# A gated H3 convolution and shifted-MLP mixer on one core: transposes moved to DMA, sums and table arithmetic spread over ScalarE and GpSimd, a filter input moved to another buffer, the instruction order tuned anew

## The chip, the cores and the metric

The kernel runs on one core of a Trainium2 chip. The metric is the device time of that core in microseconds (us). Before the change it is 277.49 us, the median of three runs (275.71 to 279.33).

The engines are called as the profile calls them: PE is TensorE (matrix products, and transposes done as products with an identity matrix), PEld its weight loads, DVE is VectorE, ACT is ScalarE, POOL is GpSimd, and SP is SyncE, whose queue starts the DMA transfers. "L547" is line 547 of the kernel in question. Line numbers differ between kernels, so each reading says what the line does.

A run counts as slow when it is more than 1.5% above the fastest run of the same kernel.

## The reference

Inputs are sequences of S = 2048 positions with D = 640 channels, in bf16. Two branches are mixed by a gate.

```python
g = sigmoid((q * gate_w).sum(-1, keepdims=True))
# branch a: H3 convolution
k_shift = sum over t of k shifted by t * shift_k        # 4 taps
kv  = k_shift * v
y   = irfft(rfft(pad(kv)) * rfft(pad(ssm_k)))[:S] + kv * ssm_D
a   = q * y
# branch b: MLP with token shifts
h   = gelu(layernorm(q) @ w1)                           # layer norm 1
hs  = concat(shift of four channel groups by +1, -1, +2, -2) @ w2
x1  = q + hs
b   = x1 + gelu(layernorm(x1) @ w3) @ w4                # layer norm 2
out = g * a + (1 - g) * b
```

## The kernel before

The Fourier transform is done as products in two steps. Step 1 multiplies 16 slabs (a slab is 128 positions by 640 channels) by a table of sines `F1`, once for the filter (`h1`) and once for `kv` (`x1`). Step 2 multiplies by a small table `M3`; then come the spectral products, the inverse of step 2 (`pv`) and the inverse of step 1 (`iv`, with the table `I1`, which is `F1` transposed). "The last spectral product" below means the last matmul of step 2 and its inverse. What follows it, called the tail here, is the inverse `iv`, the rest of W3 and W4, and the stores.

A small list scheduler, which runs while the kernel is built, decides in which order each engine executes all this. Every operation has an estimated duration and a rank. The rank is the latest start that the work behind it allows, lowered to a hand-set target time where there is one. Where an operation has alternatives (`{V: ..., A: ...}`), the scheduler chooses the engine too.

```python
LAT = 70.0                     # ns between an end and the start that depends on it, any pair of engines
TG = {"trh": us(lambda a: 4 + a), "W1": us(lambda c: 10 + 6 * c), "h1": us(lambda s: 24 + 1.2 * s),
      "W3": us(lambda c, f: 50 + 36 * c + 1.5 * f), "W4": us(lambda c, i: 70 + 36 * c + 4 * i), ...}   # cut
n.rank = min((s.rank - LAT for s in n.succ), default=400000.0) - dur
if n.tgt is not None:
    n.rank = min(n.rank, n.tgt)
```

Layer norm: the sums of a slab, then mean and 1/sqrt for two slabs at a time, the normalised slab `XN`, and its transposition to `XNT` as PE products, two slabs (10 transposes) at a time.

```python
def ln_slab(i, s, dep):                                  # i = 0: layer norm 1, i = 1: layer norm 2
    if i == 0:   # VectorE: two bn_stats and one bn_aggr
        st = pl.add("st", {V: 2 * dve(DH) + 200}, f_st, dep)
    else:        # ScalarE: Square with accum_out (the plain sum came with the W2 addition)
        st = pl.add("sq", {A: act_s(D) + 60}, ..., dep)
    # i == 1: three small VectorE operations (mean, variance); then two on GpSimd: + 1e-5, pow(-0.5)
    xn = pl.add("xn", {V: 360}, ...)                     # (x - mean) * rs
def ln_pair(i, c, i0, xns, xb):                          # both layer norms
    tr = pl.add("tr", {PE: 10 * 66}, f_tr, ...)          # nc.tensor.transpose x10
    return evac("te", ...)                               # PSUM -> XNT, on ScalarE or VectorE
```

The buffers that matter:

```python
KV  = big.tile([P, T1, D], BF16)                         # v slabs, then kv
RK  = big.tile([P, 12800], BF16)
HT  = RK[:, 0:10240]                                     # the filter, transposed: input of h1
KRG = RK[:, 0:8960]; ACC = RK[:, 8960:10240]             # k slabs and sums of the four-tap shift
TMP = RK[:, 10240:12800]
kb  = Buf(r_kr, hpe)                                     # k loads wait for every filter product (hpe)
```

So `k` cannot be loaded, and the four-tap shift products on VectorE cannot begin, before all 32 filter products of step 1 are done. (The name `HT` means the transposed filter and not its spectrum; the wording of the prediction, "spectra in the value slabs", means this buffer.)

The rest that the change touches: the token shifts of the mixed channels (`mx`) are copies on VectorE. The twiddle transposes (`tri`, `F1` to `I1`) are 32 PE transposes and two copies out of PSUM, the memory that PE writes to. The scalings of the residual (`xo`), the angles of the sine table and the mask tables are all on VectorE.

## Time and profile before

| Reading | Value |
|---|---|
| Time, median of three runs | 277.49 us |
| Span of the profiled run | 275.1 us |
| PE busy | 231.0 us |
| DVE busy | 222.9 us |
| PE idle before / after the last spectral product | 28.7 / 15.4 us |

The page's first parts, before: busy time of each engine with its share of the span, then busy tenths in 40 equal slices (one slice is 6.9 us), where `PEclk` is the granted PE clock in tenths.

```profile
span 275.1 us, 4562 instructions
PE 231.0 (84%) x1757; PEld 136.2 (50%) x1757; DVE 222.9 (81%) x419; ACT 148.5 (54%) x182; POOL 25.9 (9%) x59
...
PE   3479989799999999989989789978989699992950
...
PEclk9999999999999999999999999999999999998695
```

PE is busy for 84% of the span. It cannot finish earlier than its 231 us of work, and 44 us beside that are idle. The row `PE` shows where: at the start, in the 70% slices, and in a hole near the end (2, 9, 5, 0), where the clock falls as well.

Windows of the kernel before: start and end, length, then busy time and instruction count of PE, PEld, DVE, ACT and POOL, the granted clock, the DMA share and GB/s. The first two lines split the run at the last spectral product, at 231.95 us.

```profile
0.00:231.95 231.95, 203.25 (x1588) 119.05 (x1589) 198.67 (x382) 146.93 (x181) 25.86 (x59) 1.00 0.61 214
231.95:275.10 43.15, 27.74 (x171) 17.18 (x170) 24.20 (x37) 1.53 (x2) 0.00 (x0) 0.85 0.75 259
94.00:120.00 26.00, 24.82 (x168) 15.70 (x166) 25.62 (x42) 11.01 (x17) 3.94 (x5) 1.00 0.37 115
```

Ahead of the split PE works 203.25 of 231.95 us, so 28.7 us are idle. Behind it PE has only 27.74 us of work, and this takes 43.15 us: 15.4 us are idle. The third line is the stretch of the shift products, where DVE is busy for 25.62 of 26.00 us.

Groups of instructions, before, by line and shape: busy us, mean ns of one, then the idle time just before them with its releaser.

```profile
L547 PE MATMUL PS<-IDN,XN 128*128 128x128 bf16 x160 | 12.3, 225 | 2.0 <-DVE XNT L348 1.9
L842 PE MATMUL PS<-IDN,F 128*128 128x128 bf16 x32 | 2.1, 219 | 0.1
...
L512 DVE BATCH_NORM_STATS2 ST<-QX 128x6 f32<-128x320 bf16 x32 | 13.6, 467 | 0.0
...
L516 ACT ACTIVATE RG<-QX 128x640 bf16<-128x640 bf16 x16 | 11.8, 736 | 11.8 <-DVE QX L684 10.4 <-issue 1.4
...
L530 POOL TENSOR_TENSOR RS<-VE,NHALF 128x2 f32<-128x2 f32 x16 | 12.7, 797 | 1.3
```

These price what moves: 160 layer-norm transposes cost PE 12.3 us (80 of them, 6.15 us, belong to layer norm 2), the twiddle transposes 2.1 us. One summing pass over a slab costs ScalarE 736 ns, one `pow` costs GpSimd 797 ns.

### The profile page before, as it was taken

Reading aid. Unit: us, or ns where it says so; the run is one execution under the profiler, and the core shown is the slowest. Engines: PE = TensorE matmul, PEld = TensorE weight load, DVE = VectorE, ACT = ScalarE, POOL = GpSimd, SP = SyncE. Lnnn points to the kernel's source line nnn. Section 1 sums busy time; section 2 is a strip of 40 time slices with the busy share of each in tenths; the row PEclk is TensorE's granted clock in tenths of the full one; section 3 lists DMA queues with packets and bytes.
Section 4 is the critical chain, followed back from the end, with each engine's and each line's share of the span. In section 5 each row is a group of like instructions: output and inputs, shape, how many; then the busy total and the mean of one; then the engine's idle time right before and its main releaser. Section 6 shows DMA issues by size and latency. Waiting matters only on the chain.

```text
span 275.1 us, 4562 instructions
## 1 busy us (share of the span) xinstructions
PE 231.0 (84%) x1757; PEld 136.2 (50%) x1757; DVE 222.9 (81%) x419; ACT 148.5 (54%) x182; POOL 25.9 (9%) x59
## 2 busy tenths in 40 slices
PE   3479989799999999989989789978989699992950
PEld 4465455456664546754456543334645244761620
DVE  6989999959988999999999595999488926164694
ACT  1479969987765461374632384889276964100000
POOL 6143220010520221100000000000000000000000
PEclk9999999999999999999999999999999999998695
DMA  7999604069990040492043999959959610699954
GB/s 261 397 362 299 257 2 191 2 223 386 396 355 26 2 167 0 133 324 96 31 162 89 354 342 297 357 204 313 377 149 387 222 67 0 200 389 379 339 150 166
DMA packets 32790, 60.90 MB, mean 221 GB/s; under 512 B 2305, under 2 KB 19458, under 8 KB 32385
## 3 DMA queue, kind: packets, MB, share of 16 engines
q1 hardware_dynamic: 32768, 60.63, 62.9%
q8 instruction: 13, 0.21, 0.3%
q14 instruction: 9, 0.07, 0.1%
HBM read 37.03 MB, written 18.35 MB: 201 GB/s over the span
## 4 chain that ended last, share of the span: by engine, by line
PE 48%; DVE 26%; DMA 10%; ACT 9%; issue 5%; SPq 1%; POOL 0%; DVEq 0%; ACTq 0%; POOLq 0%
PE PS L763 17%; PE PS L775 14%; PE PS L580 4%; DMA CJ<-in_A_q_dram 4%; DMA RK<-in_A_k_dram 3%; DMA RK<-GHD 3%; PE PS L677 3%; PE PS L731 3%; PE PS L856 3%; DVE RK L823 2%; DVE W L426 2%; DVE SX L348 2%; ACT RG L767 2%; ACT SX L344 2%; DVE QX L781 2%
## 5 line engine op out<-in xcount | busy, mean ns | idle before, releaser
L775 PE MATMUL PS<-W,RG 128*128 128x320 bf16 x384 | 56.0, 305 | 2.0 <-DVE SX L348 1.1
L763 PE MATMUL PS<-XNT,W 128*128 128x512 bf16 x240 | 54.1, 379 | 1.7 <-ACT RG L767 1.0
L344 ACT CAST SX<-PS 128x640 bf16<-128x640 f32 (+1 forms) x56 | 41.1, 784 | 22.6 <-PE PS L731 22.5
L775 PEld LDWEIGHTS <-RG 128*128 128x128 bf16 x384 | 38.3, 100 | 19.3 <-issue 3.6
L763 PEld LDWEIGHTS <-W 128*128 128x128 bf16 x240 | 23.2, 98 | 30.4 <-issue 4.8
L767 ACT ACTIVATE RG<-PS 128x1024 bf16<-128x1024 f32 x24 | 24.5, 1022 | 22.5 <-PE PS L763 22.3
L781 DVE SCALAR_TENSOR_TENSOR QX<-PS,ZG,QX 128x640 bf16<-128x640 f32 x16 | 14.1, 882 | 19.8 <-PE PS L775 19.8
L348 DVE CAST SX<-PS 128x640 bf16<-128x640 f32 (+1 forms) x28 | 24.9, 903 | 1.0 <-PE PS L856 1.0
L677 PE MATMUL PS<-R 128*128 128x320 bf16 x160 | 24.0, 299 | 0.9 <-DVE ZG L606 0.3
L916 DVE TENSOR_TENSOR SX<-SX,R 128x2048 bf16<-128x2048 bf16 x20 | 23.8, 1220 | 0.7 <-PE PS L856 0.5
L580 PE MATMUL PS<-XNT,R 128*128 128x512 bf16 x100 | 22.2, 379 | 0.0
L827 DVE TENSOR_TENSOR RK<-RK 128x1280 bf16<-128x1280 bf16 x24 | 19.7, 822 | 0.5
L856 PEld LDWEIGHTS <-M 64*64 64x64 bf16 x320 | 8.9, 105 | 22.1 <-issue 14.6
L677 PEld LDWEIGHTS <-R 128*128 128x128 bf16 x160 | 15.6, 98 | 8.2 <-issue 2.0
L823 DVE TENSOR_TENSOR RK<-RK,CJ 128x1280 bf16<-128x1280 bf16 x24 | 19.6, 818 | 0.0
L731 PEld LDWEIGHTS <-F 128*128 128x128 bf16 x128 | 12.3, 97 | 12.2 <-issue 7.3
L344 ACT COPY XNT<-PS 128x1280 bf16<-128x1280 bf16 x13 | 16.0, 1232 | 4.0 <-PE PS L547 3.9
L516 ACT ACTIVATE RG<-QX 128x640 bf16<-128x640 bf16 x16 | 11.8, 736 | 11.8 <-DVE QX L684 10.4
L344 ACT CAST KV<-PS 128x1024 bf16<-128x1024 f32 x14 | 14.1, 1023 | 7.4 <-PE PS L856 7.2
L856 PE MATMUL PS<-RK,M 64*64 64x512 bf16 x160 | 13.4, 387 | 5.4 <-DMA RK<-GHD 2.4
L957 DVE SCALAR_TENSOR_TENSOR RK<-PS,ZG,CJ 128x640 bf16<-128x640 f32 x16 | 13.3, 877 | 4.4 <-DMA CJ<-in_A_q_dram 4.4
L350 DVE TENSOR_SCALAR R<-PS 128x1024 bf16<-128x1024 f32 x11 | 13.0, 1219 | 4.7 <-PE PS L856 4.5
(95 smaller groups left out, 299.1 us busy)
## 6 DMA issues: line engine op xcount, KB each, us to landing
GHD<-SX SPq DMA_DIRECT2D x8, 640.0 KB, 5.4
GXD<-SX SPq DMA_DIRECT2D x8, 640.0 KB, 3.3
RK<-GHD SPq DMA_DIRECT2D x4, 1280.0 KB, 8.8
R<-R SPq DMA_DIRECT2D x8, 640.0 KB, 8.0
RK<-GXD SPq DMA_DIRECT2D x4, 1280.0 KB, 7.6
VD<-KV SPq DMA_DIRECT2D x4, 1280.0 KB, 6.1
RK<-VD SPq DMA_DIRECT2D x8, 640.0 KB, 5.9
W<-in_B_w_dram SPq DMA_DIRECT2D x2, 1920.0 KB, 11.2
```

The costliest lines, as they stand in the source:

```text
L344: nc.scalar.copy(out=o, in_=i)
L348: nc.vector.tensor_copy(out=o, in_=i)
L580: nc.tensor.matmul(ps(pb)[:, j, :], lhsT=lhsT, rhs=XNT[:, xb.idx, k, :], start=(k == 0), stop=(k == DT - 1))
L677: nc.tensor.matmul(ps(pb)[:, j, 0:DH], lhsT=gst_ap(k, s), rhs=W2[:, k, j * DH:(j + 1) * DH], start=(k == 0), stop=(k == DT - 1))
L731: nc.tensor.matmul(ps(pb)[:, j, 0:DH], lhsT=F1[:, s, h, :], rhs=src[:, s, ds], start=True, stop=not dterm)
L763: nc.tensor.matmul(ps(pb)[:, j, :], lhsT=W3[:, k, (f0 + j) * P:(f0 + j + 1) * P], rhs=XNT[:, xb.idx, k, :], start=(k == 0), stop=(k == DT ...
L767: gns.append(pl.add("g2.%d.%d" % (c, f0), {A: act_p(1024)}, lambda e, f0=f0, pb=pb, gb=gb: nc.scalar.activation(out=GTP[:, gb.idx, f0 % 4: ...
L775: nc.tensor.matmul(ps(pb)[:, j, 0:DH], lhsT=GTP[:, gbs[f // 4].idx, f % 4, i * P:(i + 1) * P], rhs=W4[:, f, j * DH:(j + 1) * DH], start=(f ...
L823: m = pl.add("km%d.%d.%d" % (c, u, j), {V: dve(2 * D, .52)}, lambda e, src=src, cj=cj, tb=tb: nc.vector.tensor_tensor(out=TMP[:, tb.idx].r ...
L827: prev = pl.add("ka%d.%d.%d" % (c, u, j), {V: dve(2 * D, .52)}, lambda e, tb=tb: nc.vector.tensor_tensor(out=acc, in0=acc, in1=TMP[:, tb.i ...
L856: nc.tensor.matmul(pt[64 * C:64 * C + 64, R, :], lhsT=M3[64 * R:64 * R + 64, m, :], rhs=rhs_fn(R, C), start=start, stop=stop)
L916: nc.vector.tensor_tensor(out=PQ[:, qb.idx], in0=XS[:, sb.idx].unsqueeze(1).to_broadcast([P, 2, 1024]), in1=HH[:, hhb.idx, u], op=ALU.mult)
```

## The change

The intent is to relieve PE and VectorE, the two busiest engines, with engines that have room (ScalarE at 54%, GpSimd at 9%, the DMA queue at 62.9% of its engines' time):

- Layer norm 2's 80 transposes and the 32 twiddle transposes become DMA transposes. Layer norm 1 keeps PE transposes.
- Layer norm 1's sums may run on ScalarE (two summing passes) or VectorE, as the scheduler picks. The mean and variance of layer norm 2 go to GpSimd.
- Angles may run on GpSimd, and so may the copies of the shift coefficients; the mask tables do. The scalings `xo` may run on ScalarE.
- The token shifts of the mixed channels become small DMA copies.
- The transposed filter `HT` moves from `RK` into `KV`, so `k` loads and shift products no longer wait for the filter products. The `v` loads now wait for them instead.
- The scheduler changes too: other hand-over latencies, a new target for the `kv` products, four settings (`keep`, `evac`, `vpen`, `mpen`), and targets whose odd values look like the result of a search.

The diff, cut to its core (cuts marked `...`):

```diff
-LAT = 70.0
+def lat_of(n):
+    return 230.0 if "PE" in n.alts else (60.0 if n.bytes else 170.0)
...
-    TG = {"trh": us(lambda a: 4 + a), "W1": us(lambda c: 10 + 6 * c), ... }
+PAR = {
+    "trh": (-602.97, -1.2), "W1": (-11.87, 12.07, -4.15), "h1": (-36.96, 5.52), "W2": (1.53, 2.52),
+    "W3": (284.34, -0.66, -0.95), "W4": (27.62, 66.24, 29.05), "x1": (225.73, -0.37), "h2": (309.29, 2.1, 1.28),
+    "x2": (430.37, -0.29, 0.64), "pv": (93.48, 0.63, 0.03), "iv": (205.62, 6.17), "kv": (376.91, -0.47),
+    "keep": (0.07,), "evac": (1.85,), "vpen": (43.36,), "mpen": (14.32,),
+}
...
+    XTD = {(1, c) for c in range(4)}
+    LN1A = {s for s in range(T1)}
-    HT = RK[:, 0:10240].rearrange("p (t d) -> p t d", t=T1)
+    HT = KV
...
-            st.append(pl.add("ang%d" % t1, {V: dve(256)}, ...
+            st.append(pl.add("ang%d" % t1, {V: 397, G: 700}, f_ang, [c_w, c_s, c_o]))
...
+            else:                                             # ScalarE: sum and sum of squares
+                if i == 0:
+                    nc.scalar.activation(out=JNK if i else JN0, in_=QX[:, s, :], func=ACT.Copy, accum_out=SSM[:, s:s + 1])
+                nc.scalar.activation(out=JNK if i else JN0, in_=QX[:, s, :], func=ACT.Square, accum_out=SSQ[:, s:s + 1])
+        st = pl.add("st%d.%d" % (i, s), {V: 1000, A: 1470} if i == 0 and s in LN1A else ({V: 1000} if i == 0 else {A: 735}),
+                    f_st, dep)
+        # mean, variance and pow: five GpSimd operations for a pair of slabs summed on ScalarE, two otherwise
...
     def ln_pair(i, c, i0, xns, xb):
+        if (i, c) in XTD:
+            return [pl.dma("xt%d.%d.%d" % (i, c, i0 + j), lambda e, j=j: nc.sync.dma_start_transpose(
+                out=XNT[:, xb.idx, :, (i0 + j) * P:(i0 + j + 1) * P], in_=XN[:, xns[j][1].idx, :]), P * D * 2,
+                [xns[j][0]], [xb, xns[j][1]], rate=XT_RATE) for j in range(2)]
...
-                nc.vector.tensor_copy(out=GST[a:b, 4, lo:hi, 1:129], in_=MIX[a:b, lo - sh:hi - sh, :])
+                nc.sync.dma_start(out=GST[a:b, 4, lo:hi, 1:129], in_=MIX[a:b, lo - sh:hi - sh, :])
...
-        xo[s] = pl.add("xo%d" % s, {V: 296}, ...
+        xo[s] = pl.add("xo%d" % s, {V: 296, A: act_s(D)}, ...
...
-        kb = Buf(r_kr, hpe)
+        kb = Buf(r_kr)
...
-                    P * 4 * D * 2, [], [], after=15000.0)
+                    P * 4 * D * 2, hpe[8 * c:8 * c + 8], [], after=18000.0)
...
-        tr = pl.add("tri%d" % h, {PE: 16 * 58}, f_ti, f1n + [n_idn, m3n], [pb], mode="f", after=12000.0)
+    i1n = [pl.dma("tri%d" % h, lambda e, h=h: nc.sync.dma_start_transpose(
+        out=I1[:, h], in_=F1[:, h].rearrange("p t c -> p (t c)")), P * P * T1 * 2, f1n + [m3n], [], rate=XT_RATE, after=60000.0) for h in range(2)]
```

## The prediction

> **What bounds the kernel now.** The profile page gives a span of 275.1 us with TensorE (PE) busy 231.0 us (84%), VectorE (DVE) 222.9 (81%), ScalarE (ACT) 148.5 (54%), GpSimd 25.9 (9%). The chain of waits is 48% PE and 26% DVE. So PE is the floor and 44 us of idle can be won beside it. The stretch table places that idle: 9.6 us in the first 20 us, about 7 us up to 120, 1.8 in 120–148, 10.6 in 148–220, nothing in 220–244, and 15 us after 244. DVE is 99% busy in 94–148 (shift products and their adds), and the granted clock falls to 0.81 and 0.76 only in that last part.
>
> **Removed from PE.** Layer norm 2's 80 transposes (half of the 12.3 us group) and the 32 twiddle transposes (2.1): 8.2 us. PE falls to about 223 us.
>
> **Removed from DVE.** Half of the batch-norm statistics (8.5 us of 16.9), the mixing shifts (5.4), half of the angles (3.4), mask-table arithmetic (2.5), the small mean/variance operations (3.9), 14 of 16 scalings of QX (4.8): about 28 us.
>
> **Added.** ACT: eight slabs with two summing passes of 0.92 us each (736 ns plus a 188 ns accumulator read), 15 us, and 14 scalings, 9 us; minus about 12 us of transposed-tile and twiddle copies. It ends near 160 us. GpSimd: angles, tables, four coefficient copies and five instead of two operations per ScalarE-type pair; from the 327 and 797 ns of its instructions about 2.1 us a pair, 60 us in all. DMA: 18 transposes and 22 small shift copies. The small 160 KB stores land in 3.9 us, so I cost a slab transpose at 3 to 4 us of latency. [...]
>
> **What is on the critical path.** The PE work (8.2 us) is, wholly. DVE's relief pays in its saturated stretch. Spectra in the value slabs free RK, so the key loads and shift products start in the layer norm 1 stage instead of after 74 us. The instruction order shows the larger matter: after the last spectral product the old PE order has 27 us of work, and took 43 us; the new one keeps 40 us (50 of layer norm 2's W3 products, five W4 slabs) to interleave with the inverse. I expect PE work of 183 us before that point, 20 to 24 us of idle instead of 28, then about 45 us. That sums to 250 us; I add 4 for DMA contention and late GpSimd results and 2 for the difference of span and measured time.
>
> **Prediction: 256 us, 247 to 267 in 8 of 10. Chances: faster 0.93, same 0.06, slower 0.01.**
>
> **Signs that it is right.** PE busy near 223 and 87–89% of the span; DVE near 195; ACT near 160; no DVE stretch at 99%; shift products before 50 us; less than 8 us of PE idle in the last 40 us; W3 rarely waits for a transposed tile.
>
> **What would make it wrong.** Transposes that take over 6 us, or hold the queue, so that W3 or the spectral reads wait. GpSimd late for layer norm 1[...]. Shift copies stuck behind the 3.8 MB weight loads. Then the gain shrinks to 2–4%.

183 + 22 + 45 us make 250, and 4 and 2 more make 256. The 2 are the distance of the time before (277.49 us) from the span of the profiled run (275.1), rounded; the 4 were an allowance, worked out from no trace.

## More of the kernel before

What PE waited for, before: the waiting line, the releaser, us in total, times, longest.

```profile
PE PS L952 <- DVE RK L957: 5.0, 2, 4.5
```

Those are the inverse products in the tail. They wait for VectorE to free an output buffer, with nothing else left for PE to do.

## The result, and the profile after

| Kernel | Median | Range | Runs |
|---|---|---|---|
| before | 277.19 us | 275.71 to 279.33 | 4 |
| after | 255.31 us | 254.59 to 257.39 | 4 |

The ratio is 0.9217, with a 95% interval of 0.9136 to 0.9299. Here and below, a ratio is the mean time of one kernel's fast runs over that of the other's of the same rounds, so it is not quite the ratio of the medians that are quoted.

The page's first parts, after, with its DMA packet line and the line of the main queue (packets, MB, share of 16 engines):

```profile
span 252.8 us, 4384 instructions
PE 223.6 (88%) x1628; PEld 129.9 (51%) x1645; DVE 194.6 (77%) x308; ACT 154.2 (61%) x210; POOL 59.3 (23%) x144
...
PE   3858949999799999898698999969899999999993
...
PEclk9986997999999999999799999997999999999999
...
DMA packets 50069, 65.10 MB, mean 258 GB/s; under 512 B 19584, under 2 KB 36737, under 8 KB 49664
...
q1 hardware_dynamic: 50048, 64.82, 80.1%
```

The hole at the end of the row `PE` is gone. A new weakness shows near the start: the clock falls in slices 3, 4 and 7 (and briefly in 20 and 28). The queue, at 62.9% before, is at 80.1%.

Windows of the kernel after, with the same columns as before. The first two lines are split at its last spectral product, at 211.83 us.

```profile
0.00:211.83 211.83, 187.19 (x1397) 107.16 (x1413) 169.56 (x271) 148.02 (x204) 59.33 (x144) 0.96 0.81 255
211.83:252.80 40.97, 36.42 (x232) 22.71 (x234) 25.00 (x38) 6.18 (x7) 0.00 (x0) 0.99 0.79 273
94.00:120.00 26.00, 24.11 (x146) 14.35 (x147) 23.37 (x35) 16.80 (x24) 0.14 (x1) 1.00 0.57 143
74.00:94.00 20.00, 19.94 (x129) 12.44 (x128) 19.90 (x38) 16.95 (x33) 13.71 (x25) 1.00 1.00 252
...
16.00:20.00 4.00, 3.80 (x20) 1.99 (x20) 3.44 (x10) 2.73 (x6) 3.83 (x9) 0.60 1.01 339
20.00:24.00 4.00, 3.81 (x22) 2.55 (x21) 3.87 (x9) 3.70 (x9) 3.63 (x13) 0.55 0.81 257
```

From the first two lines of each kernel, with the idle time worked out as length minus PE busy, the whole difference of the spans is a sum of four terms (us):

| | before | after | difference |
|---|---|---|---|
| PE busy, up to the last spectral product | 203.25 | 187.19 | −16.06 |
| PE idle, up to there | 28.70 | 24.64 | −4.06 |
| PE busy, after it | 27.74 | 36.42 | +8.68 |
| PE idle, after it | 15.41 | 4.55 | −10.86 |
| span | 275.10 | 252.80 | −22.30 |

PE lost 7.4 us of work in sum and 14.9 us of idle. (17 of the 1645 PE records are missing from this trace, 6 of W1 and 11 of W3, and none from that of before. Their neighbours overlap, so less than 1 us of work is counted as idle for it.) Most of that idle was in the tail. There PE has 8.7 us more work than before (W3 and W4 that were kept for it) and yet finishes sooner. This table is the measuring rod of the experiments: a part of the change is known by the term that it moves.

First and last starts of the first shift product of a pair of slabs on VectorE, before (L818) and after (L870), with the durations ns min/median/max. The kernel before:

```profile
L818 DVE TENSOR_TENSOR RK<-RK,CJ x8: 815/818/825, 83.9 to 142.5; 128x1280 bf16<-128x1280 bf16 x8
```

The kernel after:

```profile
L870 DVE TENSOR_TENSOR RK<-RK,CJ x8: 814/818/825, 39.8 to 114.8; 128x1280 bf16<-128x1280 bf16 x8
```

They start 44 us earlier and end 28 us earlier. Experiment 4 shows how much of this is due to moving `HT`.

The DMA transposes of layer norm 2, after: how long an issue held the SyncE queue (ns, min/median/max), with first and last start; below, the time from issue to landing.

```profile
L593 SPq DMA_TRANSPOSE XNT<-XN x16: 1200/1430/3736, 66.8 to 154.5; - x16
...
  DVE XN L586: 4.4, 2
...
DMA to landing us min/median/max: 2.4/4.6/10.2
```

A plain load of `v` held the queue for 0.35 to 0.53 us. W3 waited for none of the transposes. VectorE did, twice, for 4.4 us in sum: a normalised slab could not be overwritten before its transpose had landed. What PE waited for, after, its longest waits (the first is for the filter to be loaded, and took 4.1 us in the kernel before):

```profile
PE PS L761 <- DMA RG<-in_A_ssm_k_dram: 4.2, 1, 4.2
PE PS L783 <- ACT KV L379: 3.4, 1, 3.4
PE PS L783 <- DVE QX L833: 2.8, 3, 2.3
...
PE PS L899 <- DMA RK<-GHD: 1.3, 1, 1.3
```

Groups of the kernel after that answer to those shown before:

```profile
L783 PE MATMUL PS<-KV,F 128*128 128x320 bf16 x128 | 26.7, 337 | 9.4 <-ACT KV L379 3.4 <-DVE QX L833 2.8 <-DVE XNT L383 2.4
L634 PE MATMUL PS<-XNT,R 128*128 128x512 bf16 x94 | 24.1, 392 | 1.3 <-DVE XNT L383 1.0
...
L579 POOL TENSOR_TENSOR RS<-VE,NHALF 128x2 f32<-128x2 f32 x16 | 13.1, 818 | 1.3
L601 PE MATMUL PS<-IDN,XN 128*128 128x128 bf16 x80 | 7.1, 245 | 1.6 <-DVE XN L586 1.4 <-ACT SX L379 0.2
L560 ACT ACTIVATE R<-QX 128x640 bf16<-128x640 bf16 x7 | 5.2, 741 | 0.0
```

The PE transposes of layer norm are down to 80. `L560 x7` shows that the scheduler gave 7 of the 16 slabs of layer norm 1 to ScalarE. L783 is step 1 of both transforms, 337 ns a product, where each half took 298 to 299 ns before: part of it ran while the clock was low (15 of the 128 products between 16.8 and 23.6 us, at a granted clock of 0.50).

### The profile page after: what moved, and what is told of

It is laid out like the page before. It is cut to its first block, busy times and chain, and to the rows that moved or that the text cites. A ratio compares the mean times of both kernels' runs of the same rounds, so it can differ in the third digit from the quotient of the medians.

```text
span 252.8 us, 4384 instructions
## 1 busy us (share of the span) xinstructions
PE 223.6 (88%) x1628; PEld 129.9 (51%) x1645; DVE 194.6 (77%) x308; ACT 154.2 (61%) x210; POOL 59.3 (23%) x144
## 2 busy tenths in 40 slices
DMA packets 50069, 65.10 MB, mean 258 GB/s; under 512 B 19584, under 2 KB 36737, under 8 KB 49664
## 3 DMA queue, kind: packets, MB, share of 16 engines
q1 hardware_dynamic: 50048, 64.82, 80.1%
## 4 chain that ended last, share of the span: by engine, by line
PE 52%; DVE 14%; DMA 13%; ACT 12%; issue 5%; POOL 2%; DVEq 0%; ACTq 0%
PE PS L827 16%; PE PS L815 14%; PE PS L728 6%; PE PS L783 5%; DMA RK<-GXD 4%; PE PS L899 4%; DMA RK<-GHD 4%; DVE RK L1000 3%; PE PS L634 3%; PE PS L761 2%; DMA KV<-in_A_v_dram 2%; DMA CJ<-in_A_q_dram 2%; DVE QX L833 2%; ACT KV L379 1%; DMA RG<-in_A_ssm_k_dram 1%
## 5 line engine op out<-in xcount | busy, mean ns | idle before, releaser
L827 PE MATMUL PS<-W,RG 128*128 128x320 bf16 x384 | 54.9, 299 | 1.7 <-ACT RG L819 0.8
L379 ACT CAST SX<-PS 128x640 bf16<-128x640 f32 (+1 forms) x54 | 39.6, 769 | 20.2 <-PE PS L899 13.3
L783 PE MATMUL PS<-KV,F 128*128 128x320 bf16 x128 | 26.7, 337 | 9.4 <-ACT KV L379 3.4
L383 DVE CAST SX<-PS 128x640 bf16<-128x640 f32 (+1 forms) x30 | 26.6, 911 | 5.1 <-PE PS L899 4.6
L634 PE MATMUL PS<-XNT,R 128*128 128x512 bf16 x94 | 24.1, 392 | 1.3 <-DVE XNT L383 1.0
L783 PEld LDWEIGHTS <-F 128*128 128x128 bf16 x128 | 13.4, 107 | 15.6 <-issue 9.0
L586 DVE TENSOR_SCALAR XN<-QX,MV,RS 128x640 bf16<-128x640 bf16 x32 | 13.8, 454 | 8.5 <-DMA XNT<-XN 4.4
L1000 DVE SCALAR_TENSOR_TENSOR RK<-PS,ZG,CJ 128x640 bf16<-128x640 f32 x16 | 13.6, 879 | 8.4 <-PE PS L995 6.2
L385 DVE TENSOR_SCALAR R<-PS 128x1024 bf16<-128x1024 f32 x10 | 11.8, 1218 | 10.2 <-PE PS L899 10.2
L379 ACT CAST KV<-PS 128x1024 bf16<-128x1024 f32 x18 | 17.7, 1027 | 0.0
L899 PEld LDWEIGHTS <-M 64*64 64x64 bf16 x320 | 8.7, 109 | 16.8 <-issue 9.7
L749 ACT ACTIVATE QX<-QX,ZG 128x640 bf16<-128x640 bf16 x14 | 11.3, 828 | 9.4 <-DVE XN L586 9.4
```

Of the source, the lines that this page charges most:

```text
L379: nc.scalar.copy(out=o, in_=i)
L383: nc.vector.tensor_copy(out=o, in_=i)
L634: nc.tensor.matmul(ps(pb)[:, j, :], lhsT=lhsT, rhs=XNT[:, xb.idx, k, :], start=(k == 0), stop=(k == DT - 1))
L783: nc.tensor.matmul(ps(pb)[:, j, 0:DH], lhsT=F1[:, h, s, :], rhs=src[:, s, ds], start=True, stop=not dterm)
L827: nc.tensor.matmul(ps(pb)[:, j, 0:DH], lhsT=GTP[:, gbs[f // 4].idx, f % 4, i * P:(i + 1) * P], rhs=W4[:, f, j * DH:(j + 1) * DH], start=(f ...
L1000: nc.vector.scalar_tensor_tensor(out=GY[:, yb.idx].rearrange("p (j d) -> p j d", j=2), in0=ps(pb)[:, :, 0:DH], scalar=G32[:, s:s + 1], in1 ...
```

## The experiments

Two theories stood against each other. Theory "work": the gain comes from the work taken off PE and VectorE. Theory "order": it comes from the new order of the instructions, so the tail has work to interleave. A third question was which of the many parts count.

An experiment that changes the work also changes what the scheduler does with it. In the runs marked "re-searched" the target times of the changed kernel were searched again with the scheduler's own model; else a kernel would be judged with targets that were made for another one. Such a run therefore changes a part and the order. The searches went unequally far: those of e4, e5 and e8 ended with one number of the targets changed (`W2` 2.52 to 2.61), that of e7 with two, while those of e2, e6 and the two calibrated kernels ended with quite other targets. Experiment 8 measures how far a different order alone scatters the time. All kernels gave correct results. Medians are of four runs each, ratios are against the kernel before in the same rounds; before had medians of 277.26, 276.76 and 277.76 us in the three groups of runs, slow runs included. In the third group (e5, e2_cal_t, x1 and c1) three of the seven runs of before were slow, and the record calls the verdict of these four kernels against before unclear; it calls e1_old_sched the same as before, and the others faster. Most of what follows compares medians of kernels with each other.

### 1. New work, old order: e1_old_sched

```diff
-    return 230.0 if "PE" in n.alts else (60.0 if n.bytes else 170.0)
+    return 70.0
-    "trh": (-602.97, -1.2), "W1": (-11.87, 12.07, -4.15), ...
+    "trh": (4.0, 1.0), "W1": (10.0, 6.0, 0.0), ...          # the targets of before; extra settings neutral
```

> The work of the changed kernel, ordered by the settings of the kernel before (its targets, its one 70 ns latency, no PSUM slots kept back). Theory W (the moved work makes the gain): near 258 us, 254 to 263, since TensorE still has 8 us less to do and VectorE 28 us less. Rival S (the retuned order makes most of the gain): 266 to 275 us, PE busy unchanged near 224 us, with the lost time as PE idle in the last 45 us as before.

Measured: 276.11 us, ratio 0.9941 [0.9848, 1.0034] (one of the four runs, 277.27 us, was slow). All of the moved work, under the old order, is worth 1.2 us by the medians, and the interval reaches past 1: it can't be told from nothing. Windows of this kernel, split at its last spectral product:

```profile
0.00:228.29 228.29, 197.12 (x1472) 114.56 (x1487) 179.81 (x280) 147.38 (x203) 57.22 (x152) 0.97 0.75 236
228.29:271.30 43.01, 26.87 (x160) 16.97 (x160) 23.53 (x37) 1.01 (x1) 0.00 (x0) 0.79 0.76 260
```

PE busy fell to 224.0 us, as in the kernel after. But the tail still has only 26.87 us of work in 43.01 us, as before the change, and its longest waits are the old ones:

```profile
PE PS L995 <- DVE RK L1000: 8.0, 3, 5.1
```

L995 is the inverse product, L1000 the VectorE operation that reads it: the wait of 5.0 us in the kernel before, grown to 8.0. In these two profiled runs PE has 7.0 us less work than before and 3.2 us more idle (47.3 us against 44.1). This run was the fastest of the four; by the medians even less of the removed work shows in the time.

### 2. Old work, new order: e2_old_work_t

The kernel before, with the scheduler of the kernel after and re-searched targets:

```diff
-LAT = 70.0
+def lat_of(n):
+    return 230.0 if "PE" in n.alts else (60.0 if n.bytes else 170.0)
-    TG = { ... }
+PAR = {"trh": (-1504.66, 61.8), "W1": (-338.17, 81.67, -6.96), ... }
```

> The work of the kernel before, ordered by the new list scheduler with its targets searched anew for this graph. Theory W: 272 to 279 us, hardly better than before. Rival S: 260 to 266 us, PE busy near 231 us, with most of the fall out of the last 45 us. Mixed: 266 to 272.

Measured: 268.59 us, ratio 0.9712 [0.9651, 0.9773]. The order alone gives 8.7 us. Its windows:

```profile
0.00:224.03 224.03, 193.23 (x1498) 110.88 (x1511) 185.96 (x367) 149.67 (x189) 24.02 (x59) 0.97 0.63 222
224.03:266.40 42.37, 37.58 (x247) 24.08 (x248) 25.82 (x40) 4.73 (x5) 0.00 (x0) 1.00 0.76 264
```

The tail now has 37.58 us of PE work and 4.8 us of idle, as in the kernel after. So the tail belongs to the order, and neither theory covers the whole gain alone: this kernel has the good tail with the old work, and e1_old_sched has the bad one with the new work. Under this kind of order the moved work is worth 268.59 − 255.31 = 13.3 us, where under the old it could not be told from nothing.

### 3. Transposes back on PE: e4_all_pe_t

```diff
-    XTD = {(1, c) for c in range(4)}
+    XTD = set()
-    i1n = [pl.dma("tri%d" % h, ... dma_start_transpose ...
+        tr = pl.add("tri%d" % h, {PE: 16 * 58}, f_ti, ...   # 32 PE transposes, as before; targets re-searched
```

> The changed kernel with layer norm 2's transposes and the twiddle transposes back on TensorE and their copies back on ScalarE or VectorE, targets searched anew. If removed PE work is worth its full length: 255.3 plus 8, 263 us. If DMA transposes cost something elsewhere (queue order, DMA time), less: 256 to 260, and SyncE's queue waits shrink. If they also relieved evacuation engines: over 265.

Measured: 261.73 us, ratio 0.9464 [0.9406, 0.9522], so 6.4 us slower than the kernel after. PE busy is 228.6 us, 5.0 more than after. That it isn't 8.2 more is in part the clock: the mean granted clock was 0.978 in this profiled run, and 0.965 in that of the kernel after. The main queue of this kernel:

```profile
q1 hardware_dynamic: 35136, 61.15, 68.3%
```

This gives an estimate of what the transposes cost the queue. Share times span is 80.1% of 252.8 us = 202.5 us with them, and 68.3% of 259.6 us = 177.3 us without: 25.2 us for 64.82 − 61.15 = 3.67 MB (16 slabs and two blocks of twiddles), or about 146 GB/s. There are 19584 DMA packets under 512 B with these transposes and 4672 without.

### 4. The filter back in RK: e6_ht_rk_t

```diff
-    HT = KV
+    HT = RK[:, 0:10240].rearrange("p (t d) -> p t d", t=T1)
-        kb = Buf(r_kr)
+        kb = Buf(r_kr, hpe)                                 # and the same for ACC and TMP; v loads wait no more; re-searched
```

> The changed kernel with the filter spectra input back in RK, so that key loads and shift products wait for the filter's first step again; targets searched anew. If the early shift products matter: 261 to 268 us with a VectorE stretch at 95 to 99% after 94 us. If not: 254 to 258.

Measured: 263.74 us, ratio 0.9546 [0.9475, 0.9617], so 8.4 us slower than the kernel after. This is the largest effect of a single part that was measured, but only 2.0 us more than that of experiment 3, which is within the scatter (experiment 8). The shift products of this kernel, and its stretch of 94 to 120 us and its first part up to the last spectral product:

```profile
L882 DVE TENSOR_TENSOR RK<-RK,CJ x8: 815/819/826, 69.9 to 129.4; 128x1280 bf16<-128x1280 bf16 x8
```

```profile
94.00:120.00 26.00, 23.57 (x134) 13.06 (x134) 25.69 (x37) 18.86 (x27) 5.26 (x7) 1.00 0.55 177
0.00:217.14 217.14, 185.83 (x1385) 104.95 (x1399) 167.34 (x268) 149.06 (x203) 56.73 (x142) 0.96 0.78 248
```

The products start at 69.9 us instead of 39.8, so moving `HT` makes 30 of the 44 us by which they start earlier. VectorE is full in 94 to 120 us again (25.69 of 26.00 us, against 25.62 before the change and 23.37 after), but not in 120 to 148 us (19.33 of 28.00 us, against 27.66 before and 16.88 after). DVE has all its other reliefs in this kernel. PE busy stays at 223.5 us, while the idle ahead of the last spectral product is back at 31.3 us (24.64 after). The 6.7 us there are most of the 8.4.

### 5. Tables, mixing shifts and sums back on VectorE: e7_tables_dve_t, e8_mix_dve_t, e5_ln1_dve_t

Three kernels, each with one relief of VectorE taken back, each re-searched:

```diff
 # e7_tables_dve_t: angles, mask tables on VectorE; coefficient copies on VectorE or ScalarE
-            st.append(pl.add("ang%d" % t1, {V: 397, G: 700}, f_ang, [c_w, c_s, c_o]))
+            st.append(pl.add("ang%d" % t1, {V: dve(256)}, ...
 # e8_mix_dve_t
-                nc.sync.dma_start(out=GST[a:b, 4, lo:hi, 1:129], in_=MIX[a:b, lo - sh:hi - sh, :])
+                nc.vector.tensor_copy(out=GST[a:b, 4, lo:hi, 1:129], in_=MIX[a:b, lo - sh:hi - sh, :])
 # e5_ln1_dve_t
-    LN1A = {s for s in range(T1)}
+    LN1A = set()
```

> The changed kernel with angles, mask tables and coefficient copies back on VectorE (copies also on ScalarE); GpSimd keeps the layer norm arithmetic; targets searched anew. VectorE gets about 7 us more work, GpSimd about 19 us less. If VectorE relief pays: 258 to 262. If GpSimd was late for layer norm 1 (its chain stood between 26 and 33 us in the changed kernel): 252 to 255, and the idle of TensorE in the first 54 us falls below 12 us.

> The changed kernel with the mixing shifts back on VectorE (5.4 us more there, 22 small transfers less on the queue); targets searched anew. If VectorE relief pays: 257 to 261. If the small transfers behind the weight loads cost as much as they free: 253 to 256.

> The changed kernel with all of layer norm 1's sums on VectorE; targets searched anew. If half of them on ScalarE pays through VectorE's relief (7 us of statistics): 258 to 262 us. If ScalarE's two passes and GpSimd's five operations a pair cost as much as they free: 253 to 257.

| Kernel | Time | Against after | Ratio to before |
|---|---|---|---|
| e7_tables_dve_t | 254.21 us | −1.1 us | 0.9197 [0.9128, 0.9267] |
| e8_mix_dve_t | 257.80 us | +2.5 us | 0.9332 [0.9280, 0.9383] |
| e5_ln1_dve_t | 253.53 us | −1.8 us | 0.9169 [0.9093, 0.9244] |

None of the three costs more than the scatter of the order (experiment 8), and two of the kernels are a little faster than the one that was shipped. One by one, these reliefs can't be seen in the time. The 2.5 us of e8_mix_dve_t are just within that scatter, and its time lies in the range that was expected if the relief pays, so this one stays open. The test is also weaker than it looks, for the scheduler moved other work in turn: VectorE was busy for 197.1, 199.6 and 194.0 us in the three kernels, against 194.6 after. In e5_ln1_dve_t the sums are back, but VectorE makes 22 instead of 30 of the copies into `SX`, and is no busier. All three put back together were not tested.

### 6. Latencies alone: f1_lat70_t

The kernel after, with the old 70 ns between any two operations in the scheduler's model, re-searched:

```diff
-    return 230.0 if "PE" in n.alts else (60.0 if n.bytes else 170.0)
+    return 70.0
```

> The changed kernel's work and scheduler, but with the one 70 ns hand-over latency of the kernel before in the model; the targets searched anew under it. If the latencies themselves carry the gain of the ordering: 264 us or more. If the searched targets carry it: 253 to 259 us, near the changed kernel's 255.

Measured: 258.33 us, ratio 0.9349 [0.9283, 0.9416], 3.0 us slower than after. That is the size of the scatter (2.7 us). So the gain of the order comes mostly from targets that fit the work, and not from the new latencies; whether these add a microsecond or two is left open. (This search ended close to the shipped targets, which had been found with the new latencies.)

### 7. Durations from the trace: g1_cal_t and e2_cal_t

The scheduler plans with durations that the trace shows to be too short: a pair of GpSimd mean and `pow` operations is planned at 1.05 or 1.5 us and takes about 2.3 (435 + 304 + 287 + 472 + 818 ns), an issue of a DMA transpose at 0.06 and takes 1.43, a normalised slab at 0.36 and takes 0.45. These two kernels plan with durations set from the traces, one with the new work and one with the old, both re-searched:

```diff
-DMA_ISSUE = 60.0
+DMA_ISSUE = 380.0                                            # and 1400 / 2900 for the DMA transposes
-    return 55.0 + 0.833 * n
+    return 120.0 + 0.875 * n                                 # ScalarE; similarly VectorE
-            rsn[(i, s0)] = pl.add("rs%d.%d" % (i, s0), {G: 1050 if i == 0 else 1500}, f_rs, [st, n_idn])
+            rsn[(i, s0)] = pl.add("rs%d.%d" % (i, s0), {G: 2000 if i == 0 else 2300}, f_rs, [st, n_idn])
```

> The work of the changed kernel, nothing moved between engines; only the durations in the scheduler's table set to those of the changed kernel's trace (a 1.4 us hold of SyncE for a slab transpose, 2.0 to 2.3 us of GpSimd per layer norm pair, 1.87 us for two summing passes), targets searched anew. If order is what is left to win: 246 to 252 us with PE busy unchanged near 224. If the durations don't matter: 254 to 257.

> The work of the kernel before, the new scheduler, durations set from the traces, targets searched anew: the best order I can give the old work. Against the 250.5 us of the new work ordered the same way. If the moved work is worth 8 us of TensorE time or more under a good order: 259 to 267 us. If order was nearly all: 252 to 258.

Measured: g1_cal_t 250.51 us (248.32 to 251.84), ratio 0.9060 [0.8987, 0.9132]; it beats both kernels. e2_cal_t 263.68 us, ratio 0.9539 [0.9457, 0.9621]. The difference of the two is 13.2 us, as that of experiment 2 and the kernel after (13.3). (The four kernels were not all timed in the same rounds; from their ratios to before, the differences are 0.0479 and 0.0495 of some 277 us, 13.3 and 13.7 us.) The pages of the two kernels, busy times and the granted clock in slices; first e2_cal_t:

```profile
PE 225.6 (86%) x1741; PEld 133.0 (51%) x1757; DVE 211.2 (81%) x406; ACT 160.1 (61%) x196; POOL 23.1 (9%) x59
...
PEclk9999999979999999999999999999999999999999
```

Then g1_cal_t:

```profile
PE 217.2 (87%) x1629; PEld 126.5 (51%) x1645; DVE 195.1 (78%) x304; ACT 155.4 (62%) x218; POOL 52.8 (21%) x151
...
PE   0199998998999989988998989899699999999874
...
PEclk9999999999999999999999999999999999999999
```

Both keep the granted clock for longer than the kernel after, so here the PE work can be compared at nearly one clock: 225.6 − 217.2 = 8.4 us. Of this, the slice at 0.7 in e2_cal_t (3.4 us at half clock) can account for up to 1.7 us. By groups, the layer-norm and twiddle transposes take 12.6 + 2.1 us in e2_cal_t and 6.9 in g1_cal_t, 7.8 us less, where they were priced at 8.2. (g1_cal_t was expected to keep PE busy near 224 us; it has 217.2.) g1_cal_t lets PE start late (its first product is at 11.68 us, after 11.68 us of idle) and then has no long pause; the four runs had a mean granted clock of 1.0, 0.993, 0.993 and 1.0, where those of the kernel after had 0.964 to 0.972. These figures leave out the start. The record of the clock begins only at 16.8 us in g1_cal_t, 16.7 in before and 9.9 in after, and the time ahead of it is counted as full clock. The pace of PE says otherwise: 16 filter transposes took 1.91 us at 12.7 us and 1.17 us at 21.9 us in g1_cal_t, and 1.88 us at 13.4 us and 1.18 us at 17.2 us in before. So a late start does not keep PE at full pace from its first product.

### 8. The control: c1_jitter

The kernel after with its targets moved a little at random, the work unchanged. 97 of the 221 PE steps stand elsewhere, and the scheduler's model thinks this order 0.7% longer.

```diff
-    "trh": (-602.97, -1.2), ..., "W2": (1.53, 2.52), "W3": (284.34, -0.66, -0.95), ...
+    "trh": (-602.97, -0.99), ..., "W2": (1.53, 2.0), "W3": (284.34, 4.43, -0.95), ...
```

> Control: the work and scheduler of the changed kernel, its targets jittered at random (97 of 221 TensorE steps stand at another place; the scheduler's own model holds it as 0.7% longer). What a mere reshuffle does: 254 to 260 us expected, whichever theory holds; differences of this size between the other kernels are then not evidence.

Measured: 258.02 us, ratio 0.9332 [0.9248, 0.9416], 2.7 us slower than after. This is the ruler for the runs above: a re-searched kernel within 2.7 us of another has shown nothing. It is one draw only, so the ruler is rough. The 6.4 us of experiment 3 and the 8.4 of experiment 4 are well beyond it, and so are 8.7 and 13.3.

### 9. The lost clock: x1_fifth_copy

After the filter's transposes PE pauses for 3.40 us at 11.9 us, until the last of five copies is done on ScalarE, and from 16.8 to 23.6 us it runs at half clock. This kernel keeps the order of the kernel after and moves only that copy to VectorE, to shorten the pause.

```diff
+    for n in plan:
+        if n.name == "trh0":
+            n.start = 8500.0
+        elif n.name == "trhe0":
+            n.eng, n.start = "DVE", 8626.0
+    plan = sorted(plan, key=lambda n: (n.start, n.seq))
```

> The changed kernel with its instruction order kept and one instruction moved: the last of the five copies of transposed filters goes from ScalarE to VectorE, so that TensorE's pause between the filter transposes and the first filter product (11.9 to 15.3 us) should shrink from 3.4 to about 2 us. If the halved clock seen after that pause (0.60 and 0.55 of full speed from 16 to 24 us) comes from a pause of that length: the clock there returns to 1.00, TensorE's busy time falls by 3 to 4 us, and the time to 250 to 254 us. If the clock falls for another reason: still 0.5 to 0.6 in that stretch, 254 to 257 us.

Measured: 256.37 us, ratio 0.9281 [0.9181, 0.9381]; not faster. The pause became shorter, and the clock fell all the same. PE's timeline of this kernel (start, length, instructions, idle before), and its windows from 10.47 us on:

```profile
14.40 0.43 PE L783 MATMUL PS<-KV,F 128*128 128x320 bf16 x1 [2.58 <-DVE KV L383]
```

```profile
10.47:13.88 3.41, 1.36 (x20) 1.16 (x18) 2.59 (x9) 3.17 (x3) 3.06 (x10) 1.00 1.06 386
13.88:17.29 3.41, 2.88 (x8) 0.80 (x8) 3.34 (x10) 0.69 (x1) 3.19 (x4) 0.50 1.03 396
17.29:20.71 3.42, 2.57 (x16) 1.62 (x16) 3.35 (x10) 2.25 (x5) 3.17 (x10) 0.50 1.03 325
20.71:24.12 3.41, 3.41 (x20) 2.27 (x18) 3.38 (x7) 2.77 (x6) 3.12 (x11) 0.50 0.60 169
```

So this theory, that the length of the one pause of 3.4 us takes the clock, is not confirmed. Here the clock fell although the pause was only 2.58 us, and the half clock lasted 10.2 us, in which PE was busy for 8.9.

The clock records of the 14 kept traces show what goes with a fall. In all of them the granted clock changes on a grid of 3.41 us. On this grid, 45 windows at full clock were followed by half clock, and PE was busy in them for 1.85 us at most. Of the 912 that were followed by full clock, only six had PE busy for 1.85 us or less (1.52 to 1.79). (In the traces of before and after alone, up to the end of PE's work, five windows at full clock were followed by half clock, with PE busy for 0.85 to 1.46 us, and 130 by full clock, with PE busy for at least 1.78.) So in these runs a fall goes with a window in which PE works for less than about half of the time, and not with one pause of a given length. This fits x1_fifth_copy: the pause is shorter, but the window from 10.47 us still has only 1.36 us of work (1.46 in the kernel after, from 13.35 us). It fits g1_cal_t too, where no window from 16.8 us to the end of PE's work has less than 1.9 us of work. What ends the half clock is left open: in e4_all_pe_t PE was busy for all of 16.19 to 19.60 us at half clock, and the clock stayed at half until 23.02 us.

## Why the prediction was right or wrong

The four terms of the time, for every kernel where they decide something (us; up to and after the last spectral product; idle is length minus PE busy):

| Kernel | Work | Order | Busy, up to | Idle, up to | Busy, after | Idle, after | Span |
|---|---|---|---|---|---|---|---|
| before | old | old | 203.25 | 28.70 | 27.74 | 15.41 | 275.1 |
| e1_old_sched | new | old | 197.12 | 31.17 | 26.87 | 16.14 | 271.3 |
| e2_old_work_t | old | new | 193.23 | 30.80 | 37.58 | 4.79 | 266.4 |
| after | new | new | 187.19 | 24.64 | 36.42 | 4.55 | 252.8 |
| e4_all_pe_t | new, transposes on PE | new | 179.81 | 25.39 | 48.75 | 5.65 | 259.6 |
| e6_ht_rk_t | new, filter in RK | new | 185.83 | 31.31 | 37.63 | 6.33 | 261.1 |
| e2_cal_t | old | new, calibrated | 186.15 | 30.99 | 39.49 | 4.77 | 261.4 |
| g1_cal_t | new | new, calibrated | 175.85 | 25.73 | 41.32 | 6.10 | 249.0 |

The table is of single profiled runs (that of e1_old_sched was its fastest, 3 us below its median), so the medians decide on the times and the table on where they lie.

**The time: right.** 256 us was predicted, 247 to 267, and 255.31 was measured. The sum behind it was 183 us of PE work up to the last spectral product, 20 to 24 of idle, and 45 for the rest; measured were 187.2, 24.6 and 41.0. Two terms are off by 4 us and cancel, and the 4 us that were added for DMA contention and GpSimd stand for losses that came mostly from elsewhere (below), so that the sum is this close by luck.

**"The PE work (8.2 us) is, wholly" on the critical path: right only under the new order.** In the two calibrated kernels the transposes take 7.8 us less of PE (experiment 7), and the transposes put back cost 6.4 us (experiment 3). Under the old order the same removal, with everything else that was moved, gained 1.2 us, which can't be told from nothing (experiment 1). So the engine that is the floor on average (PE, busy for 84% of the span before) lost nothing measurable by this work under an order in which it waited elsewhere. PE busy of 223.6 us against a forecast of 223 looks exact, but is a balance, and so in part luck: 8.2 us of transposes were removed; the low clock made the first products slower (step 1 took 28.1 us with its constant term, where before it took 24.7; W1 at least 24.1, with 6 of 100 records missing, where before 22.2), and in the tail, with a granted clock of 0.99 against 0.85 before, the inverse products were faster (9.8 us against 10.9 for the 64 of them).

**"Spectra in the value slabs free RK": right, and the largest single effect measured.** Shift products were foretold before 50 us and came at 39.8. Experiment 4 undoes this, with the order searched anew: 8.4 us, and 6.7 us of PE idle come back ahead of the last spectral product. Its price, the `v` loads that must now wait for filter products, was not foreseen: the last is issued only at 108.6 us, and the chain of waits holds such a load for about 5.1 us.

**"DVE's relief pays in its saturated stretch": this step failed, as far as it was tested.** VectorE busy fell to 194.6 us as foretold (195), and in 94 to 148 us from 53.28 to 40.25 us. But tables, mixing shifts and sums, put back one at a time, cost nothing beyond the scatter (experiment 5). Experiments 3 and 4 add up to 14.8 us, more than the 13.3 us of all the moved work, so if the parts simply add, nothing that could be measured is left for the reliefs of VectorE. With the filter back in `RK` and all the reliefs in place, 94 to 120 us is as full as ever, and the time is 8.4 us longer. What paid there was mainly earlier work: the shift products begin at 39.8 instead of 69.9 us. How much the reliefs thinned the stretch beyond that was not separated. The sign "no DVE stretch at 99%" is wrong as well. A full stretch stands at 74 to 94 us now, with 19.90 of 20.00 us busy. It costs no PE time there, since PE is busy for 19.94 us.

**"The instruction order shows the larger matter": right.** The tail was to have less than 8 us of PE idle, and has 4.55. Experiments 1 and 2 show that this comes from the order alone. The prediction read this from the order of the instructions but did not say whose doing it was, the work's or the scheduler's.

**Why 22 us is more than the parts.** The order alone gives 8.7 us, the work alone 1.2, both together 22. The order gives the tail back in any case (10.6 us of idle, with e2_old_work_t). The work gives 7.2 us of PE busy and 6.2 us of idle ahead of the last spectral product, but only if PE has other work ready whenever it is freed. In the old order that idle is 28.7 us without the moved work and 31.2 us with it.

**"I add 4 for DMA contention and late GpSimd results": present, but the loss was mostly elsewhere.** Layer norm 1 does wait for GpSimd: the chain of waits has `pow` pieces in it between 27.2 and 33.1 us. Landing took 4.6 us in the median, up to 10.2, against 3 to 4. Neither made W3 or the spectral reads wait for a transpose. What was not predicted is the clock, 0.60 and 0.55 in 16 to 24 us: PE was busy for 6.6 us of the 6.8 us at half clock, and ten layer-norm transposes took 1.25 us there (at 18.92 us) and 0.72 us at full clock (at 28.66 us). If all of this work took half as long at full clock, its cost would be 3.3 us of PE time, at the pace of the transposes 2.8; both are estimates. Calibrated durations with a late, unbroken start of PE won 4.8 us (experiment 7).

**What would have made it wrong.** The transposes did hold the SyncE queue for 1.43 us each, 3.7 at worst; no wait of PE is put down to one. GpSimd worked 59.3 us, as foretold (60), and its `pow` took 818 ns against 797 before; where layer norm 1 waited for it stands above.

**Not tested alone:** the residual scalings on ScalarE, and layer norm 2's mean and variance on GpSimd. Each re-searched kernel also changes the order, and its search may have been shorter than the one behind the shipped targets.

## What to carry to other kernels

Work taken from the busiest engine is worth what the order makes of it: the same removal was worth 1.2 us, within the noise, under an order made for the old work and 13.3 under one searched for the new, so re-tune the order before you judge a change, and measure a jittered order as a ruler for what a microsecond means. Look first for what holds back the start of the work in a saturated stretch: here another buffer for one input was worth 8.4 us, and none of the reliefs that were put back singly was worth more than the scatter. Split the span at the last point that everything must pass, and count busy and idle of the bottleneck on both sides: it tells at once which of two causes a gain belongs to.
